# Batch 0 of a Fourier-mixing and gated-FFN kernel: first chunk pair by pair, a new float64 conversion, loads in order of need

## The chip, the cores and the metric

The kernel runs on one core of a Trainium2 chip. The metric is the time of one execution in microseconds (us). The median before the change was 2103.89 us over three runs (2100.69 to 2103.98). Every timed run of this study fell in the fast state. Runs taken once, without rounds, have an unknown state and are named as single runs.

Engine names as the profile has them: PE is TensorE, PEld its weight loads, DVE VectorE, ACT ScalarE, POOL GpSimd, SP SyncE. A trailing q (ACTq) is that engine's instruction stream, not its arithmetic. "PEclk" is the granted TensorE clock as a share of full speed.

## The reference

```python
x: (8, 3008, 256) float32                       # batch, sequence, features
X   = real(fft(fft(x, axis=1), axis=2))         # mixing over sequence, then features
t   = X.reshape(8 * 3008, 256)
out = (sigmoid(t @ w_gate) * (t @ w_val)) @ w_out
# w_gate, w_val: (256, 1536); w_out: (1536, 256); all three arrive as float64
```

## The kernel before

TensorE sums over the sequence with cosine and sine tables ("sequence sums", tiles `ev`, `od`). The feature transform is merged into the gate and value weights (`merge`, tiles `ps`, `pe`, results `G1`, `G2`, `ge`). Then every batch is worked off in chunks of 256 sequence positions. A chunk has six *pairs* of hidden blocks, each pair has two *halves*: `front` (four matmuls into `pa`, four into `pb`), the sums on VectorE, a sigmoid on ScalarE, gating on VectorE and GpSimd, and four halves later `back` (matmuls into `po`).

Before any pair can run, x and the tables have to land, x has to be folded, the sequence sums of batch 0 have to run, and the float64 weights have to become float32 and be merged. The order of batch 0, with cuts marked:

```python
load_x(0)                                        # two halves of x
nc.scalar.dma_start(out=dt, ...)                 # feature table
for t in range(2):
    nc.scalar.dma_start(out=st[:, t], in_=stab[:, t])     # sequence tables
...
for f in fold_ops(0, nc.vector, NQ): f()
seq_start(0)
for blk in range(2):
    for what in range(3):
        seq_group(0, blk, what)()                # 12 sequence sums
load_weights()                                   # all 18 weight tiles, then merged
load_x(1)
e_load()                                         # column 128 of batches 1 to 7
```

One weight tile of 128x512 numbers was converted so (`hi`, `lo` are the two 32-bit words of a float64):

```python
ts(out=expi, in0=hi, scalar1=0x7FF00000, ...)                    # VectorE
nc.gpsimd.tensor_scalar(out=exp, in0=expi, ... mult, add)        # GpSimd: new exponent
nc.gpsimd.tensor_scalar(out=expi, in0=exp, ... max, min)         # GpSimd: clamp
ts(out=mani, in0=hi, ... and, shift)                             # VectorE
ts(out=mani, in0=mani, scalar1=0x3F800000, ... or)               # VectorE
stt(out=man, in0=lo, scalar=2.0 ** -52, in1=man, mult, add)      # VectorE
nc.gpsimd.tensor_tensor(out, man, exp, op=ALU.mult)              # GpSimd
stt(out=out, in0=hi, scalar=-(2 ** 31), in1=out, and, or)        # VectorE: sign
```

The other part that matters is the load of feature column 128 (`HD`), which later batches need on its own. Seven loads, each of 126 x 4 x 6 = 3024 pieces of four bytes, are issued by ScalarE:

```python
def e_load():
    for b in range(1, B):
        nc.scalar.dma_start(out=x8[:, b - 1], in_=xf[b, :, :, :, HD : HD + 1])
```

## Time and profile before

| | before |
|---|---|
| median of 3 runs | 2103.89 us |
| span of the profiled run | 2099.9 us |
| busy: TensorE, VectorE, GpSimd, ScalarE | 96%, 85%, 65%, 23% |
| mean granted clock | 0.984 |
| front of half 10 starts (landmark of the prediction) | 168.47 us |

The busy shares are averages, and they hide where the idle time lies. TensorE's 4% of idle time is about 80 us, and 69 us of it stand before 143 us. Therefore the views to read are the ones of the first 170 us: the slices, the stretch windows, the chain that ended last, and ScalarE's timeline. The prediction shows the lines.

### The profile page before, as it was taken

How to read it: one execution, taken by the hardware profiler on the slowest of the kernel's cores; microseconds unless marked ns; L12 is line 12 of the kernel's file. 1: busy time of each engine (PE TensorE's matmuls, PEld its weight loads, DVE VectorE, ACT ScalarE, POOL GpSimd, SP SyncE). 2: the span in 40 equal slices, each digit the busy share in tenths (PEclk: the TensorE clock that was granted, in tenths of full speed). 3: DMA queues.
4: the chain of work that ended last, by engine and by line, in shares of the span. 5: the costliest groups of instructions: out<-in, count | busy, mean ns of one | idle time of the engine just before them, and what ended most of it. 6: DMA issues, size and time to landing. Idle time of an engine off the chain costs nothing.

```text
span 2099.9 us, 27507 instructions
## 1 busy us (share of the span) xinstructions
PE 2020.0 (96%) x9264; PEld 1757.6 (84%) x9264; DVE 1790.4 (85%) x3263; ACT 479.0 (23%) x842; POOL 1371.0 (65%) x1663
## 2 busy tenths in 40 slices
PE   4749999999999999999999999999999999999998
PEld 2638788988898888988889888988889888898887
DVE  3979877998789978899779987899788997798887
ACT  0112222222222222222222222222222222222222
POOL 0988844687556964589446975569645894565664
PEclk9769999999999999999999999999999999999999
DMA  5350100210002000201002100020002010000001
GB/s 181 104 108 2 30 16 11 70 24 21 11 12 77 25 11 16 74 11 32 14 11 70 34 11 11 16 74 26 11 18 72 10 36 11 11 13 17 11 16 24
DMA packets 132579, 70.96 MB, mean 34 GB/s; under 512 B 124405, under 2 KB 124661, under 8 KB 130172
## 3 DMA queue, kind: packets, MB, share of 16 engines
q1 hardware_dynamic: 110608, 64.27, 10.9%
q10 hardware_dynamic: 21832, 4.94, 1.2%
q8 instruction: 74, 1.21, 0.2%
q14 instruction: 65, 0.53, 0.1%
HBM read 44.50 MB, written 24.68 MB: 33 GB/s over the span
## 4 chain that ended last, share of the span: by engine, by line
PE 74%; POOL 18%; DVE 5%; issue 2%; DMA 1%; ACTq 0%; DVEq 0%; ACT 0%; POOLq 0%
PE po L88 32%; PE pa L88 18%; PE pb L88 18%; PE ev L88 3%; PE od L88 3%; POOL sf L324 2%; POOL sf L323 2%; POOL exp L136 2%; POOL sf L321 2%; POOL sf L325 2%; DMA st<-in_stab_dram 1%; POOL x L211 1%; DVE h L319 1%; POOL x L218 1%; DVE ae L304 1%
## 5 line engine op out<-in xcount | busy, mean ns | idle before, releaser
L443 ACT ACTIVATE z<-z 128x512 f32<-128x512 f32 (+1 forms) x576 | 358.6, 622 | 1316.6 <-DVE z L308 1316.6
L304 DVE SCALAR_TENSOR_TENSOR ae<-ek,ge,pa 128x256 f32<-128x256 f32 (+1 forms) x1152 | 489.9, 466 | 194.2 <-PE pa L88 190.7
L88 PE MATMUL pa<-pk,G 128*128 128x256 f32 (+1 forms) x2304 | 583.1, 375 | 28.7 <-DVE ae L304 28.7
L88 PE MATMUL pb<-qk,G 127*128 127x256 f32 (+1 forms) x2304 | 583.5, 375 | 0.0
L88 PE MATMUL po<-sf,wf 128*128 128x256 f32 (+1 forms) x2304 | 537.4, 375 | 0.6
L88 PEld LDWEIGHTS pa<-pk,G 128*128 128x128 f32 x2304 | 438.3, 190 | 86.2 <-DVE ae L304 29.1
L88 PEld LDWEIGHTS po<-sf,wf 128*128 128x128 f32 x2304 | 435.5, 190 | 55.7 <-POOL sf L325 3.3
L88 PEld LDWEIGHTS pb<-qk,G 127*128 127x128 f32 x2304 | 437.7, 190 | 51.7
L323 POOL TENSOR_TENSOR sf<-h 128x256 f32<-128x256 f32 (+1 forms) x288 | 212.7, 738 | 398.1 <-DVE h L319 398.1
L319 DVE TENSOR_TENSOR h<-z 128x512 f32<-128x512 f32 (+1 forms) x576 | 443.8, 770 | 0.0
L307 DVE TENSOR_TENSOR z<-ae,pb 128x512 f32<-128x512 f32 (+1 forms) x576 | 390.1, 677 | 60.6 <-DVE ae L304 0.9
L88 PE MATMUL po<-h,wf 128*128 128x256 f32 (+1 forms) x1728 | 413.0, 374 | 0.0
L308 DVE TENSOR_TENSOR z<-ae,pb 128x512 f32<-128x512 f32 (+1 forms) x576 | 386.1, 670 | 0.0
L88 PEld LDWEIGHTS po<-h,wf 128*128 128x128 f32 x1728 | 327.5, 189 | 38.6
L321 POOL TENSOR_TENSOR sf<-h 128x256 f32<-128x256 f32 (+1 forms) x288 | 217.5, 755 | 214.9 <-DVE h L319 213.7
L324 POOL TENSOR_TENSOR sf<-sf,h 128x256 f32<-128x256 f32 (+1 forms) x288 | 213.9, 743 | 22.6
L325 POOL TENSOR_TENSOR sf<-h,sf 128x256 f32<-128x256 f32 (+1 forms) x288 | 213.4, 741 | 22.6
L88 PE MATMUL ev<-st,x 126*128 126x377 f32 (+5 forms) x204 | 72.3, 490 | 24.3 <-DMA st<-in_stab_dram 24.3
L360 ACT COPY c<-po 128x512 f32<-128x512 f32 (+1 forms) x144 | 78.5, 579 | 67.9 <-PE po L88 67.9
L367 DVE STREAM_TRANSPOSE os<-c 128x256 f32<-128x256 f32 x192 | 83.5, 436 | 0.0
L88 PEld LDWEIGHTS ev<-st,x 126*128 126x128 f32 (+2 forms) x204 | 37.8, 187 | 46.4 <-DVE x L212 23.4
L389 POOL TENSOR_TENSOR c<-c 128x512 f32<-128x512 f32 (+1 forms) x47 | 74.6, 1586 | 0.0
(68 smaller groups left out, 855.0 us busy)
## 6 DMA issues: line engine op xcount, KB each, us to landing
x<-in_xf_dram SPq DMA_DIRECT2D x16, 1512.0 KB
out_dram<-os SPq DMA_DIRECT2D x288, 64.0 KB
out_dram<-os SPq DMA_DIRECT2D x96, 56.0 KB
ek<-ed SPq DMA_DIRECT2D x7, 752.5 KB
st<-in_stab_dram ACTq DMA_DIRECT2D x2, 2223.7 KB
raw<-in_moe_w_gate_dram SPq DMA_DIRECT2D x6, 512.0 KB
raw<-in_moe_w_val_dram SPq DMA_DIRECT2D x6, 512.0 KB
raw<-in_moe_w_out_dram SPq DMA_DIRECT2D x6, 512.0 KB
```

What stands on the lines that cost most here:

```text
L88: nc.tensor.matmul(o, l, r, start=start, stop=stop, skip_group_check=True)
L304: nc.vector.scalar_tensor_tensor(out=ae[:, g], in0=ek[:, ks], scalar=ge[:, g, f : f + 1], in1=pa[:, g], op0=ALU.mult, op1=ALU.add)
L307: nc.vector.tensor_tensor(z[:, :, 0], ae, pb, op=ALU.add)
L308: nc.vector.tensor_tensor(z[:, :, 1, ::-1], ae, pb, op=ALU.subtract)
L319: nc.vector.tensor_tensor(h[:, fh], z[:, 0], z[:, 1], op=ALU.mult)
L321: tt(s[:, 2], h[:, 0, 0], h[:, 0, 1], op=ALU.subtract)
L323: tt(s[:, 0], h[:, 0, 1], h[:, 1, 1], op=ALU.add)
L324: tt(s[:, 1], s[:, 0], h[:, 0, 0], op=ALU.subtract)
L325: tt(s[:, 3], h[:, 1, 0], s[:, 1], op=ALU.subtract)
L360: nc.scalar.copy(t[:, 2 * j : 2 * j + 2, 0:n], PO[j][:, :, 0:n])
L367: nc.vector.transpose(os_[:, s, 0:nb, h, :], t[:, slot, 0 : nb * TB])
L443: nc.scalar.activation(z[:, 0], z[:, 0], AF.Sigmoid)
```

## The change

The intent is to let the pairs of the first chunk start while weights are still arriving. Weight tiles are reordered so that each pair's gate, value and output tiles come together; two tiles are loaded and converted first of all, three more are converted before the first half, and the other 13 inside the loop. The conversion uses three engines, with a single GpSimd instruction in place of three. x comes in three parts and the tables in four, each cut into a 112-row and a 14-row transfer. Copies of the folded x and of the output weights move from VectorE to ScalarE, and the second batch's x is loaded one chunk later. The diff, cut to its core:

```diff
-    def load_x(b):
+    def rows(out, src):
+        m = NP // 16 * 16                                  # 112 of 126 rows
+        nc.sync.dma_start(out=out[0:m], in_=src[0:m])
+        nc.sync.dma_start(out=out[m:NP], in_=src[m:NP])
+    def load_x(b, nq):
...
+    def weight_round(j):
...
+        nc.scalar.activation(ws, hi.bitcast(F32), AF.Abs)
+        nc.scalar.activation(lo, lo.bitcast(U32), AF.Copy, scale=2.0 ** -29)
+        ts(out=ws, in0=ws, scalar1=2.0 ** -15, scalar2=HUGE, op0=ALU.max, op1=ALU.min)
+        ts(out=wi, in0=wi, scalar1=3, scalar2=0x3FFFFFF8, op0=ALU.logical_shift_left,
+           op1=ALU.bitwise_and)
+        nc.vector.scalar_tensor_tensor(out=wi, in0=hi, scalar=-(2 ** 30), in1=wi,
+                                       op0=ALU.bitwise_and, op1=ALU.bitwise_or)
+        nc.gpsimd.tensor_tensor(wi, wi, lo, op=ALU.add)
...
-        nc.vector.tensor_copy(f[:, 0:2], w[:, :, 0])       # forms of w_out
+        nc.scalar.copy(f[:, 0:2], w[:, :, 0])
...
-    load_weights()
-    load_x(1)
-    e_load()
+    for j in range(2, KEEP):                               # three tiles before half 0
+        weight_round(j)
+    weight_use(2)
...
+    for c in range(1, NPR):
+        i = 2 * (c - 1)                                    # side work of halves i and i + 1
+        at(i, lambda c=c: weight_use(3 * c), lambda c=c: weight_step(3 * c + 2))
+        at(i + 1, lambda c=c: weight_use(3 * c + 1), lambda c=c: weight_use(3 * c + 2))
+        if c + 1 < NPR:
+            at(i, lambda c=c: weight_step(3 * c + 3))
+            at(i + 1, lambda c=c: weight_step(3 * c + 4))
+    i0 = 2 * NPR
+    at(i0 + 1, lambda: load_x(1, 3), e_load)               # column 128 now inside the loop
```

More of the change, by code (lines that the diff above doesn't have):

```diff
@@ L37 @@
 NP = 126
+HUGE = float((2 ** 24 - 1 - 2 ** 20) * 2.0 ** -7)
 @with_exitstack
@@ L94 @@
     X = {}
-    def load_x(b):
+    def rows(out, src):
[3 more added lines that the diff above has]
+    def load_x(b, nq):
         X[b] = xp.tile([NP, 4, NQ, D], F32, name="x4", tag="x4")
-        for h in range(2):
-            nc.sync.dma_start(out=X[b][:, 2 * h : 2 * h + 2], in_=xf[b, :, 2 * h : 2 * h + 2])
+        for q in range(0, NQ, nq):
+            rows(X[b][:, :, q : q + nq], xf[b, :, :, q : q + nq])
     dt = const.tile([P, 2, D], F32, name="dt")
@@ L109 @@
     ed = dram.tile([B - 1, NK], F32, name="ed")
-    load_x(0)
-    nc.scalar.dma_start(out=dt, in_=dtab.rearrange("(c p) d -> p c d", p=P))
-    for t in range(2):
-        nc.scalar.dma_start(out=st[:, t], in_=stab[:, t])
-    def weight_ops(src, out):
-        src = src.rearrange("(c p) f -> p c f", p=P)
-        if src.dtype == F32:
-            return lambda: nc.sync.dma_start(out=out, in_=src), lambda: None
-        raw = zp.tile([P, 2, WC, 2], I32, name="raw", tag="z")
-        man = hp.tile([P, 2, WC], F32, name="man", tag="h")
-        exp = op.tile([P, 2, WC], F32, name="exp", tag="os")
-        lo = raw.bitcast(U32)[:, :, :, 0]
-        hi = raw[:, :, :, 1]
-        mani, expi = man.bitcast(I32), exp.bitcast(I32)
-        ts = nc.vector.tensor_scalar
-        stt = nc.vector.scalar_tensor_tensor
-        def first():
-            nc.sync.dma_start(out=raw.rearrange("p c f w -> p c (f w)"), in_=src.bitcast(I32))
-            ts(out=expi, in0=hi, scalar1=0x7FF00000, scalar2=None, op0=ALU.bitwise_and)
-            nc.gpsimd.tensor_scalar(out=exp, in0=expi, scalar1=8.0, scalar2=-896.0 * 2.0 ** 23,
-                                    op0=ALU.mult, op1=ALU.add)
-            nc.gpsimd.tensor_scalar(out=expi, in0=exp, scalar1=0.0, scalar2=255.0 * 2.0 ** 23,
-                                    op0=ALU.max, op1=ALU.min)
-            ts(out=mani, in0=hi, scalar1=0xFFFFF, scalar2=3, op0=ALU.bitwise_and,
-               op1=ALU.logical_shift_left)
-            ts(out=mani, in0=mani, scalar1=0x3F800000, scalar2=None, op0=ALU.bitwise_or)
-            stt(out=man, in0=lo, scalar=2.0 ** -52, in1=man, op0=ALU.mult, op1=ALU.add)
-            nc.gpsimd.tensor_tensor(out, man, exp, op=ALU.mult)
-        def then():
-            stt(out=out.bitcast(I32), in0=hi, scalar=-(2 ** 31), in1=out.bitcast(I32),
-                op0=ALU.bitwise_and, op1=ALU.bitwise_or)
-        return first, then
@@ new lines, in load_tables, with weight_load @@
+    def load_tables():
+        for t in range(2):
+            for cs in (slice(0, NE), slice(NE, NE + NO)):
+                rows(st[:, t, :, cs], stab[:, t, :, cs])
+    jobs = [(w, c) for c in range(NPR) for w in range(3)]
+    RAW, WS = {}, {}
+    mega = []
+    KEEP = 5
+    def weight_load(j):
+        w, c = jobs[j]
+        src = (moe_w_gate, moe_w_val, moe_w_out)[w]
+        src = src[2 * c * P : 2 * (c + 1) * P, :] if w == 2 else src[:, c * WC : (c + 1) * WC]
+        src = src.rearrange("(c p) f -> p c f", p=P)
+        if j < KEEP:
+            raw = zp.tile([P, 2, WC, 2], I32, name="raw", tag="z")
+            ws = (app if j < 3 else hp).tile([P, 2, WC], F32, name="ws", tag="ae" if j < 3 else "h")
+        else:
+            if not mega:
+                mega.append(xp.tile([P, 12, 2 * WC], F32, name="mega", tag="x4"))
+            r, i = (j - KEEP) % 3 * 2, 6 + (j - KEEP) % 6
+            raw = mega[0][:, r : r + 2].rearrange("p a n -> p (a n)").bitcast(I32).rearrange(
+                "p (c f w) -> p c f w", c=2, w=2)
+            ws = mega[0][:, i].rearrange("p (c f) -> p c f", c=2)
+        WS[j] = ws
+        if src.dtype == F32:
+            nc.sync.dma_start(out=ws, in_=src)
+        else:
+            RAW[j] = raw
+            nc.sync.dma_start(out=raw.rearrange("p c f w -> p c (f w)"), in_=src.bitcast(I32))
@@ new lines, in weight_round @@
+    def weight_round(j):
+        if j not in RAW:
+            return
+        raw = RAW.pop(j)
+        lo, hi = raw[:, :, :, 0], raw[:, :, :, 1]
+        ws = WS[j]
+        wi = ws.bitcast(I32)
+        ts = nc.vector.tensor_scalar
+        nc.scalar.activation(ws, hi.bitcast(F32), AF.Abs)
[6 more added lines that the diff above has]
+        nc.gpsimd.tensor_tensor(wi, wi, lo, op=ALU.add)
@@ L149, in merge, with weight_use @@
+    def weight_use(j):
+        w, c = jobs[j]
+        (forms(WS.pop(j), c) if w == 2 else merge(WS.pop(j), w, c))
     def merge(ws, g, c):
@@ L168, in forms @@
         sub = lambda o, a, b: nc.gpsimd.tensor_tensor(o, a, b, op=ALU.subtract)
-        nc.vector.tensor_copy(f[:, 0:2], w[:, :, 0])
-        nc.vector.tensor_copy(f[:, 2], w[:, 1, 1])
+        nc.scalar.copy(f[:, 0:2], w[:, :, 0])
+        nc.scalar.copy(f[:, 2], w[:, 1, 1])
         sub(f[:, 4], w[:, 0, 1], w[:, 0, 0])
@@ L174, in forms @@
         sub(f[:, 3], w[:, 1, 0], f[:, 5])
-    def load_weights():
-        jobs = []
-        for c in range(NPR):
-            for g, w in enumerate((moe_w_gate, moe_w_val)):
-                jobs.append((w[:, c * WC : (c + 1) * WC], g, c))
-        for c in range(NPR):
-            jobs.append((moe_w_out[2 * c * P : 2 * (c + 1) * P, :], None, c))
-        rest = []
-        for src, g, c in jobs:
-            ws = app.tile([P, 2, WC], F32, name="ws", tag="ae")
-            first, then = weight_ops(src, ws)
-            first()
-            for f in rest:
-                f()
-            use = (lambda ws=ws, c=c: forms(ws, c)) if g is None else (
-                lambda ws=ws, g=g, c=c: merge(ws, g, c))
-            rest = [then, use]
-        for f in rest:
-            f()
     W = {}
@@ L205, in point, with first @@
             tt(x4[:, i, q, 1:D], x4[:, i, q, 1:D], x4[:, j, q, D - 1 : 0 : -1], op=ALU.add)
-        def first(i, j):
-            tt(x4[:, i, :, 0], x4[:, i, :, 0], x4[:, j, :, 0], op=ALU.add)
+        def first(i, j, q):
+            tt(x4[:, i, q, 0], x4[:, i, q, 0], x4[:, j, q, 0], op=ALU.add)
         def feat(v, r, q):
@@ L212, in feat, with kind @@
             tt(v[:, q, 1:HD], v[:, q, 1:HD], v[:, q, D - 1 : HD : -1], op=ALU.add)
+        parts = [(x4[:, 1 + 2 * blk], x4[:, 2 * blk]) for blk in range(2)]
         qs = [slice(q, q + nq) for q in range(0, NQ, nq)]
-        for i in (0, 2):
-            ops += [lambda i=i, q=q: point(i, i + 1, q) for q in qs]
-            ops.append(lambda i=i: first(i, i + 1))
-        ops += [lambda q=q: tt(x4[:, 1, q], x4[:, 0, q], x4[:, 2, q], op=ALU.add) for q in qs]
-        ops += [lambda q=q: tt(x4[:, 3, q], x4[:, 0, q], x4[:, 2, q], op=ALU.subtract) for q in qs]
-        for blk in range(2):
-            v, r = x4[:, 1 + 2 * blk], x4[:, 2 * blk]
+        def kind(q):
+            two = [[lambda i=i: point(i, i + 1, q)] for i in (0, 2)]
+            return two + [[lambda: tt(x4[:, 1, q], x4[:, 0, q], x4[:, 2, q], op=ALU.add)],
+                          [lambda: tt(x4[:, 3, q], x4[:, 0, q], x4[:, 2, q], op=ALU.subtract)]] + [
+                [lambda v=v, r=r: feat(v, r, q)] for v, r in parts]
+        if b:
+            for n, group in enumerate(zip(*[kind(q) for q in qs])):
+                ops += [f for fs in group for f in fs]
+                if n < 2:
+                    ops.append(lambda n=n: first(2 * n, 2 * n + 1, slice(0, NQ)))
+        else:
+            for q in qs:
+                for n, fs in enumerate(kind(q)):
+                    ops += fs
+                    if n < 2:
+                        ops.append(lambda n=n, q=q: first(2 * n, 2 * n + 1, q))
+        for blk, (v, r) in enumerate(parts):
+            W[b, blk] = (v[:, :, 0:HD], r[:, :, 0 : HD - 1])
             if b == 0:
                 we = cp.tile([NP, NQ, P], F32, name="we", tag="c7")
-                ops.append(lambda we=we, v=v: eng.tensor_copy(
+                ops.append(lambda we=we, v=v: nc.scalar.copy(
                     we, v[:, :, HD : HD + 1].to_broadcast([NP, NQ, P])))
-            ops += [lambda v=v, r=r, q=q: feat(v, r, q) for q in qs]
-            W[b, blk] = (v[:, :, 0:HD], r[:, :, 0 : HD - 1]) + ((we,) if b == 0 else ())
+                W[b, blk] += (we,)
         return ops
@@ L258, in seq_group @@
     def seq_group(b, blk, what):
-        rows = HD - 1 if what == 1 else P
-        return half(lambda q: W[b, blk][what][:, q, :], PQE[b][what], blk, what == 1, rows)
+        return half(lambda q: W[b, blk][what][:, q, :], PQE[b][what], blk, what == 1,
+                    HD - 1 if what == 1 else P)
     ER = []
@@ L395, in finish @@
             lambda: store(1)])
-    for f in fold_ops(0, nc.vector, NQ):
-        f()
+    nc.scalar.dma_start(out=dt, in_=dtab.rearrange("(c p) d -> p c d", p=P))
+    for j in range(2):
+        weight_load(j)
+    load_x(0, 2)
+    load_tables()
+    for j in range(2, KEEP):
+        weight_load(j)
+    for j in range(2):
+        weight_round(j)
+    for f in fold_ops(0, nc.vector, 2):
+        f()
+    for j in range(2):
+        weight_use(j)
     seq_start(0)
-    for blk in range(2):
-        for what in range(3):
-            seq_group(0, blk, what)()
-    load_weights()
-    load_x(1)
-    e_load()
+    for blk, what in ((0, 0), (0, 2), (1, 0), (1, 2), (0, 1), (1, 1)):
+        seq_group(0, blk, what)()
+    for j in range(2, KEEP):
+        weight_round(j)
+    weight_use(2)
+    for j in range(KEEP, KEEP + 3):
+        weight_load(j)
     per = 2 * NPR * len(chunks)
@@ L416, in split, with weight_step @@
         at(i, lambda: at(i + 1, f(*args)))
+    def weight_step(j):
+        weight_round(j)
+        if j + 3 < len(jobs):
+            weight_load(j + 3)
+    for c in range(1, NPR):
[7 more added lines that the diff above has]
+    at(i0 + 1, lambda: load_x(1, 3), e_load)
     for b in range(B - 1):
@@ L420, with folds @@
         if b:
-            at(s0 + 1, lambda b=b: load_x(b + 1))
-        def folds(s0=s0, b=b):
+            at(s0 + 1, lambda b=b: load_x(b + 1, 3))
+        f0, g0, gs = (s0 + 9, s0 + 36, 8) if b else (i0 + 9, i0 + 36, 7)
+        def folds(f0=f0, b=b):
             for j, f in enumerate(fold_ops(b + 1, nc.gpsimd, 2)):
-                at(s0 + 9 + j, f)
-        at(s0 + 8, folds)
-        at(s0 + 33, lambda b=b: seq_start(b + 1))
+                at(f0 + j, f)
+        at(f0 - 1, folds)
+        at(g0 - 3, lambda b=b: seq_start(b + 1))
         for j in range(4):
-            split(s0 + 36 + 8 * j, seq_group, b + 1, j // 2, j % 2)
-    at(20, e_fold)
-    split(26, e_rows, 0)
-    split(28, e_rows, 1)
-    at(30, e_out)
+            split(g0 + gs * j, seq_group, b + 1, j // 2, j % 2)
+    at(i0 + 22, e_fold)
+    split(i0 + 28, e_rows, 0)
+    split(i0 + 30, e_rows, 1)
+    at(i0 + 32, e_out)
     fresh = None
```

## The prediction

> **What bounds the kernel now.** I first read the busy tenths of the page and the stretch windows. Columns of a window: length, then busy us (and instructions) of TensorE, its weight loads, VectorE, ScalarE and GpSimd, then granted clock, DMA share, GB/s.
>
> ```profile
> PE   4749999999999999999999999999999999999998
> POOL 0988844687556964589446975569645894565664
> PEclk9769999999999999999999999999999999999999
> 10.00:20.00 10.00, 0.00 (x0) 0.00 (x0) 5.01 (x6) 0.00 (x0) 0.00 (x0) 1.00 0.89 319
> 80.00:90.00 10.00, 7.86 (x38) 6.95 (x38) 9.86 (x13) 2.15 (x9) 9.50 (x7) 0.81 0.36 105
> 120.00:130.00 10.00, 0.00 (x0) 0.00 (x0) 6.92 (x12) 0.00 (x0) 9.59 (x12) 0.50 0.95 276
> 160.00:170.00 10.00, 10.00 (x48) 8.79 (x47) 9.69 (x18) 2.41 (x4) 5.10 (x7) 1.00 0.00 1
> ```
>
> From about 143 us on TensorE never rests; before that it is idle or underfed. So the whole change can only act on the start. The chain that ended last says what fills it (start, us, what):
>
> ```profile
> 1.98 28.69 DMA st<-in_stab_dram
> ...
> 90.52 1.31 POOL ws L142
> 91.82 0.09 issue
> 91.91 0.69 POOL exp L134
> 92.67 2.28 POOL exp L136
> ...
> 143.10 2.08 PE pa L88 x4
> ...
> 168.47 0.86 PE pa L88 x4
> ```
>
> First the tables land (30.7 us), then twelve sequence sums on TensorE run to 50 us, then GpSimd converts 18 weight tiles at 4.5 us each (0.69 + 2.28 + 1.31 and gaps), and only at 143.1 do the pairs run. Counting two halves a pair, two fronts had been slipped in before; a pair takes 6.48 us (0.86 four times, 1.30, 1.73), and the front of half 10 starts at 168.47. That is my landmark: everything behind it stays TensorE work.
>
> Two more views. The by-form list from 51 to 142 us gives the cost of a conversion's operations (count, busy us, mean ns, idle before):
>
> ```profile
> L142 POOL TENSOR_TENSOR ws<-man,exp 128x512 f32<-128x512 f32 x18 | 23.5, 1305 | 1.5
> L140 DVE TENSOR_SCALAR man<-man 128x512 int32<-128x512 int32 x18 | 19.6, 1089 | 0.6
> L145 DVE SCALAR_TENSOR_TENSOR ws<-raw,ws 128x512 int32<-128x512 int32 x18 | 18.0, 1001 | 9.5 <-POOL ws L142 9.5
> L138 DVE TENSOR_SCALAR man<-raw 128x512 int32<-128x512 int32 x18 | 15.0, 835 | 0.0
> ```
>
> And ScalarE's timeline shows something now hidden: the seven loads of column 128 (4-byte pieces) hold its instruction stream for 26 us, beside the GpSimd chain that ends at 140.5 anyway.
>
> ```profile
> 110.90 26.25 ACTq L267 DMA_DIRECT2D x<-in_xf_dram  x7
> 137.24 1.28 ACT L443 ACT_TABLE_LOAD   x1 [26.19 <-DMA x<-in_xf_dram]
> ```
>
> **What the Trainium skill says.**
> - "SBUF — State Buffer", Who interferes with whom: VectorE in a two-port mode, or with two SBUF inputs, and GpSimd lock each other out for a whole instruction. The trace agrees: a TENSOR_SCALAR of 128x512 takes 0.42 to 0.43 us at 118.4, when it meets no lock, and 0.84 to 1.09 on average over the conversion.
> - "TensorE: Matmul & The Clock Gate", What's actually happening: the clock halves after an idle window of about 3.4 us and returns after a busy one. Here it halved about 2.4 us after TensorE stopped (114.4), and after the restart at 143.1 the 2 us windows (0.50, 0.50, 0.61, 1.00) give 4.5 us at half clock, a loss of 2.2.
> - "DMA: Bandwidth & Descriptors", Why a DMA increments its semaphore by 16: a transfer uses the largest number of engines up to 16 that divides its outer dimensions, so 126 partitions use 14. The DMA share of 0.88 to 0.89 while x and the tables stream agrees (14/16 = 0.875). The new split into 112 and 14 rows gives the busiest engine 8 rows in place of 9.
> - "ScalarE: Activation LUTs", Step-by-step: every function has the same rate per element. So Abs and Copy of 128x512 should take sigmoid's 0.62 us of this trace; no run of before has them.
>
> **The change, part by part.**
>
> *Loads.* Two weight tiles now go first, then x in three parts, then the tables in four. Until the first table quarter 0.26 + 1.05 + 3.10 + 1.14 = 5.55 MB are due; at 319 GB/s times 9/8, that is 360, plus 2.5 us: 18 us. The folds, in three parts of about 4.1 us (twelve operations at the rates of the present ones), finish at about 21; then ScalarE's copies also free the four PSUM banks the first two merges hold. The remaining tables land by 28, never late. Twelve groups of 1.90 us, plus 2.2 for the cold clock, end at about 46.5 instead of 50.
>
> *Conversion.* Per tile GpSimd drops from three operations (4.3 us) to one integer add (as L142, 1.3); VectorE from five to three (two TENSOR_SCALAR, one SCALAR_TENSOR_TENSOR: 1.6 us free of locks, from 0.45 + 0.46 + 0.69 at 118.4; 2.9 at the averages above; GpSimd now being busy some 60% instead of 95%, I take 2.3); ScalarE gains two of 0.62. Three tiles are converted before half 0: VectorE 47.5 to 54.4, then its front operations (two ae, two z, 2.3 together), the table load 1.3, sigmoid 0.63, three copies of merged weights 0.8: 59, say 58.5.
>
> *Pair by pair.* Per pair TensorE has 6.5 + two merges of 2.75 (present trace, full clock) = 12.0; VectorE 6.1 + 3 x 2.3 = 13.0; GpSimd 3 x 1.3 + forms 2.4 + gating 3.0 = 9.3; ScalarE 7.3. If these overlapped perfectly, 13 us. But the in-order lists of the changed program make a ring: ScalarE does Abs and Copy only behind the sigmoid and the merged copies of that half; VectorE does the front of the next half only behind those roundings. From the merged copies of an even half: Abs 0.7, two roundings 4.6, front 2.3, sigmoid 0.7, copies 0.9, wf copies 0.65, Abs 0.65, one rounding 2.2, front 2.3, sigmoid 0.7, copies 0.9: 16.6 us. TensorE waits in it about 4 us for the odd half's copies, enough to lose its clock; then front (cold), back, merge end 17.5 instead of 15.4 after the mark. I take 17 us a pair. Four such pairs lead to half 8: 58.5 + 68 = 126.5. Half 8 has one rounding left, half 9 none: + 0.7 + 2.2 + 2.3 + 0.7 + 0.8 = 6.7. Front of half 10: 133.2, against 168.5, 35.3 earlier.
>
> *Column 128.* Its seven loads now stand in ScalarE's list behind the sigmoid of half 13, inside the loop that TensorE bounds. Alone, one took 2.19 us (the last, behind the other traffic); seven are 15.4, less some 2.4 that stay queued: ScalarE issues nothing for about 13 us. TensorE has front 14, back 10, front 15, back 11, front 16 to do meanwhile, then needs the output banks that ScalarE empties at the chunk's end: 7.6 us of work. It resumes at about 14.7: a hole near 6.7, and 2.2 for the clock: 8.9 us given back.
>
> *Rest.* The second batch's x and folds move one chunk later, with 60 halves instead of 72 to hide in; GpSimd has room (26 to 48 of 50 us). Zero.
>
> Sum: 35.3 - 8.9 = 26.4 earlier; 2103.9 - 26.4 = 2077.5, rounded 2077.
>
> **The rivals.**
> 1. *The engines overlap as their sums allow:* 13 us a pair and no clock loss. Front 10 at 58.5 + 52 + 6 = 116.5, gain 52, less the hole 43: 2061. For it: all four sums are below 13. Against: the ring, and the locks, which in the present conversion keep VectorE at 9.86 of 10.
> 2. *The loads of column 128 cost nothing:* they queue without holding ScalarE, or are through sooner with free DMA engines; with 17 us a pair, 2069, with 13 a pair 2052. For it: in the present trace they shared the DMA with 4.7 MB. Against: the last one alone still took 2.19 us.
> 3. *The clock stays half:* TensorE needs up to 24 us of work a pair, so a pair takes 20 to 21. Front 10 at about 147, gain 21 less 9: 2092. For it: the present conversion, with gaps of 1.8 us, runs at 0.66 to 0.89. Against: gaps are fewer and the work between them denser.
> 4. *A lost overlap in steady state* (batch 0's squeezed side work): some us, nothing in the profile near its limit.
>
> **Range and chances.** The pair time (14 to 20 us, four times) is worth 24 us, the hole 5 to 12. Together 2060 to 2092. Faster by over 2% needs less than 2061.8: rival 1 or 2 nearly pure, 0.17. Slower by 2% would need new stalls of 68 us: 0.01.
>
> **What would show it.** After: sequence sums from about 21 to 46 us; conversion operations at 0.6 (ScalarE), 1.3 (GpSimd); pairs 17 us apart, with TensorE waiting on ScalarE's merged copies and a clock below 1; front 10 near 133; one gap of sigmoids of about 13 us about 13 us later, with a TensorE hole of 6 to 7 in it, waiting for ScalarE; then 100% to the end. Wrong if the pairs come every 13 us, if the integer add on GpSimd is much slower than 1.3, or if no hole follows the column loads.

## The result

The median after the change is 2075.58 us over four runs (2074.76 to 2076.9), against 2103.85 for the kernel before in the same comparison. Ratios in this document are the mean time of one kernel's fast runs over that of the other's of the same rounds, so they are not quite the ratio of the medians that are quoted. Here the ratio is 0.987, with a 95% interval of 0.9853 to 0.9887: 1.3% less time, which counts as "same" at the 2% line. The profiled spans are 2099.9 and 2072.8 us, 27.1 apart, where the prediction had 26.4. The mean clock went from 0.984 to 0.988.

The busy tenths of the page of the kernel after, in 40 slices of 51.8 us each:

```profile
PE   7789999999999999999999999999999999999998
POOL 0546944696558944687556974579545885565654
```

TensorE's first slice went from 4 to 7, the second stayed at 7, and the third went from 4 to 8. That third slice is 104 to 155 us: the old idle time before the pairs is gone from it, but it holds a new hole. GpSimd's second slice fell from 9 to 5.

TensorE's timeline shows where the sequence sums start. The bracket holds the idle time just before and what ended it:

```profile
24.83 3.83 PE L92 MATMUL ev<-st,x 126*128 126x377 f32 x6 [6.03 <-ACT ge L189]
```

They start at 24.83 (predicted 21), released by ScalarE's last copy of merged weights and not by a table. ScalarE's list has two copies of folded x ahead of the merged copies, and these could start only at 22.67, behind VectorE's folds. The folds began at 10.99 and ended at 24.9. Their first operation in VectorE's timeline, with the idle time before it:

```profile
10.99 1.42 DVE L212 TENSOR_TENSOR x<-x 126x510 f32<-126x510 f32 x1 [0.54 <-DMA x<-in_xf_dram]
```

So x was waited for only 0.54 us. Until 10.44 VectorE was still rounding the first two weight tiles, which stand ahead of the folds in its list.

The groups by line and shape between 62 and 130 us give the cost of the new conversion (count, busy us, mean ns, idle before and what ended it):

```profile
L170 POOL TENSOR_TENSOR mega<-mega 128x512 int32<-128x512 int32 x13 | 16.9, 1297 | 19.0 <-issue 9.6 <-ACT mega L164 5.8 <-DVE mega L168 3.5
L166 DVE TENSOR_SCALAR mega<-mega 128x512 int32<-128x512 int32 x13 | 10.8, 830 | 0.4
L168 DVE SCALAR_TENSOR_TENSOR mega<-mega 128x512 int32<-128x512 int32 x13 | 9.0, 692 | 0.4
L163 ACT ACTIVATE mega<-mega 128x512 f32<-128x512 f32 x13 | 9.0, 690 | 0.0
L165 DVE TENSOR_SCALAR mega<-mega 128x512 f32<-128x512 f32 x13 | 6.5, 499 | 17.7 <-ACT mega L163 15.2 <-POOL sf L347 2.5
```

GpSimd's integer add takes 1.30 us, as predicted. VectorE's three operations add up to 0.50 + 0.83 + 0.69 = 2.02 us a tile, where 2.3 was predicted. The 0.83 of L166 is a mean of unlike cases: 0.43 us where no GpSimd instruction ran beside it, 0.56 to 0.84 beside other GpSimd work, and 1.38 to 1.41 each time it fell beside the integer add of the tile before. The last row shows VectorE waiting 15.2 us in all for ScalarE's Abs.

That wait is one link of the ring that the prediction described. A piece of the chain that ended last, over one odd half (start, us, what):

```profile
99.88 0.63 ACT z L495
100.51 0.26 ACT G L187
...
101.10 0.31 ACT wf L196
...
101.61 0.59 ACT mega L163
...
102.22 0.63 DVE mega L165
...
102.88 0.57 DVE mega L166
...
103.47 0.69 DVE mega L168
104.16 0.80 DVE ae L326 x2
...
105.05 0.69 DVE z L329
105.74 0.61 DVE z L330
...
106.37 0.63 ACT z L495
```

It runs from one sigmoid to the next without TensorE: sigmoid, merged copies, copies of the output weights, Abs, rounding on VectorE, front sums on VectorE, sigmoid. Sigmoids of even halves start at 60.71, 75.40, 90.53, 106.37 and 121.63, that is 60.92 / 4 = 15.23 us a pair. The front of half 10 starts at 129.50, 39.0 us earlier than before.

Then comes the hole. ScalarE's timeline behind the sigmoid of half 13, and the chain over the same time:

```profile
142.52 0.63 ACT L495 ACTIVATE z<-z 128x512 f32<-128x512 f32 x1 [2.40 <-DVE z L330]
142.54 16.72 ACTq L289 DMA_DIRECT2D x<-in_xf_dram  x7
159.30 0.37 ACT L370 COPY c<-po 128x256 f32<-128x256 f32 x1 [16.16 <-issue]
```

```profile
143.15 0.84 ACTq L289
...
144.02 4.01 ACTq L289
...
148.06 2.23 ACTq L289
...
157.05 2.21 ACTq L289
...
159.30 0.38 ACT c L370
...
159.73 3.08 PE po L92 x6
```

ScalarE can do nothing from 143.15 to 159.26 because its instruction stream is issuing the seven loads of column 128 ("<-issue" means that the copy waited for no other engine). TensorE runs out of work, then continues at half clock. Its timeline and its stretch window (length; busy us of TensorE, weight loads, VectorE, ScalarE, GpSimd; clock; DMA share; GB/s):

```profile
159.73 3.08 PE L92 MATMUL po<-h,wf 128*128 128x256 f32 x6 [8.80 <-ACT c L370]
150.00:160.00 10.00, 1.20 (x6) 0.74 (x5) 0.00 (x0) 0.70 (x2) 0.00 (x0) 0.73 0.75 5
```

The whole path moves 5 GB/s in this window while the DMA engines are busy 75% of the time: many tiny pieces. Of the 39.0 us won by half 10, the span kept 27.1; 11.9 were given back.

### The profile page after: what moved, and what is told of

Same layout as the page of the kernel before. It is cut to its first block, busy times and chain, and to the rows that moved or that the text cites. A ratio compares the mean times of both kernels' runs of the same rounds, so it can differ in the third digit from the quotient of the medians.

```text
span 2072.8 us, 27549 instructions
## 1 busy us (share of the span) xinstructions
PE 2023.2 (98%) x9264; PEld 1757.7 (85%) x9264; DVE 1750.4 (84%) x3233; ACT 502.2 (24%) x892; POOL 1316.3 (64%) x1627
## 4 chain that ended last, share of the span: by engine, by line
PE 72%; POOL 14%; DVE 6%; issue 2%; ACTq 1%; ACT 0%; DVEq 0%; POOLq 0%
PE po L92 31%; PE pa L92 18%; PE pb L92 17%; PE ev L92 3%; PE od L92 3%; POOL sf L346 2%; POOL sf L345 2%; POOL sf L343 2%; POOL sf L347 2%; DVE ae L326 2%; DVE h L341 1%; POOL x L218 1%; POOL x L226 1%; POOL x L219 1%; DVE z L330 1%
## 5 line engine op out<-in xcount | busy, mean ns | idle before, releaser
L92 PE MATMUL od<-st,x 126*128 126x377 f32 (+5 forms) x204 | 70.1, 479 | 0.0
```

What stands on the lines that cost most here:

```text
L92: nc.tensor.matmul(o, l, r, start=start, stop=stop, skip_group_check=True)
```

## The experiments

All runs gave the right output. Runs without an interval are single ones.

Two theories stood. **Mine:** the ring of in-order lists sets the pair time, and the issue of the column loads costs some 9 to 12 us. **The rivals:** the engines' sums or the clock set the pair time; and the TensorE hole comes from something else, such as the second batch's x. A third question was whether the new loads are really faster.

### e_sp: the column loads issued by SyncE

```diff
-            nc.scalar.dma_start(out=x8[:, b - 1], in_=xf[b, :, :, :, HD : HD + 1])
+            nc.sync.dma_start(out=x8[:, b - 1], in_=xf[b, :, :, :, HD : HD + 1])
```

> The changed kernel with the seven column-128 loads issued from the sync engine's queue instead of ScalarE's. Theory A (ScalarE's instruction stream is held while its own queue issues them; 16.1 us from 143.2 to 159.3 in the changed kernel's trace): no ScalarE gap, no TensorE hole near 151 to 160, about 11.5 us less: 2062 to 2066. Rival B (the hole comes from the DMA being full, and something else that needs a DMA is late): the hole stays or moves, 2073 to 2077.

Measured: 2064.07 us (2063.06 to 2064.84), ratio 0.9816 (0.98 to 0.9833), as theory A expected. ScalarE's timeline at the place of the hole:

```profile
144.20 0.63 ACT L495 ACTIVATE z<-z 128x512 f32<-128x512 f32 x1 [2.40 <-DVE z L330]
146.60 0.37 ACT L370 COPY c<-po 128x256 f32<-128x256 f32 x1 [1.77 <-PE po L92]
147.66 0.63 ACT L495 ACTIVATE z<-z 128x512 f32<-128x512 f32 x1 [0.69 <-DVE z L330]
```

The copy follows the sigmoid by 2.4 us instead of 16.8, and the hole is gone with the same bytes and pieces moved. So it was the issue on ScalarE's stream, and its price was 2075.58 - 2064.07 = 11.5 us. SyncE's stream was held for 24.2 us instead, and TensorE did not wait for it. Whether a stream is held by the work of issuing so many pieces or by a queue that is full is not shown.

### before_e_sp: the same edit in the kernel before

The edit is the one of e_sp, made in the old kernel.

> The kernel before with the same single edit. Theory A with 'hidden behind the GpSimd chain': no change, 2102 to 2106. Rival (these loads cost the kernel before as well): 2088 to 2095.

Measured: 2102.8 us, ratio 0.9999 (0.9984 to 1.0014). In the old order the loads held ScalarE for 26 us and cost nothing, because everything waited for GpSimd's conversions until 140.5 anyway. The change moved the loads from a hidden place to an exposed one.

### ring: ScalarE's part of a conversion one half earlier

`weight_round` is cut in two. The Abs and Copy of a tile are emitted one half ahead; nothing else moves.

```diff
+    def weight_act(j):                  # Abs and Copy, once per tile
...
     def weight_round(j):
+        weight_act(j)
-        nc.scalar.activation(ws, hi.bitcast(F32), AF.Abs)
-        nc.scalar.activation(lo, lo.bitcast(U32), AF.Copy, scale=2.0 ** -29)
...
+    for j in range(KEEP, KEEP + 2):     # ahead of half 0
+        weight_act(j)
...
+            at(i, lambda c=c: weight_act(3 * c + 4))
+            at(i + 1, lambda c=c: weight_act(3 * c + 5))
+                at(i + 1, lambda c=c: weight_act(3 * c + 6))
```

> The changed kernel with the two ScalarE operations of each conversion put into ScalarE's list one half earlier, so that VectorE finds Abs done when it comes to a rounding; nothing else moved. Theory A (the ring ScalarE-VectorE-TensorE sets the 15.2 us pairs): pairs of about 13 us, the sum of VectorE's work; front of half 10 near 120 instead of 129.6; 2064 to 2068. Rival C (VectorE's locks with GpSimd set the pair): pairs stay at 14.5 to 15.5, 2073 to 2076. Rival D (TensorE's halved clock sets it): pairs stay above 15.

Measured: 2063.42 us (2061.77 to 2063.65), a little less than the 2064 to 2068 expected, ratio 0.9813 (0.9799 to 0.9828; whether that is 2% is unclear). Even sigmoids start at 61.59, 72.05, 85.14, 98.31 and 111.61. That is 50.0 us for four pairs instead of 60.9; the last three take 13.1 to 13.3 each. The front of half 10 starts at 119.02, 10.5 us earlier than in the kernel after. The waits between 62 and 122 us (who waits for what: us, times, longest), first of the kernel after and then of this run:

```profile
ACT z L495 <- DVE z L330: 34.3, 8, 5.3
DVE mega L165 <- ACT mega L163: 13.0, 7, 3.2
```

```profile
ACT z L513 <- DVE z L339: 19.8, 9, 3.8
```

VectorE's wait for Abs, 13.0 us in the first, is no longer among the waits of the second, and the sigmoid waits 14.5 us less. A stretch of one pair in this run:

```profile
85.00:98.00 13.00, 13.00 (x70) 11.63 (x69) 12.59 (x20) 6.85 (x16) 9.48 (x12) 1.00 0.39 121
```

VectorE is busy 12.59 of 13 us, and TensorE never rests and keeps its clock. This is the prediction's first rival, 13 us a pair, and it came true as soon as the ring was opened. So the ring was the bound in the kernel after, and neither the engines' sums nor the clock. (The clock has a part in the gain, because it stays full once the gaps are short. But the kernel after needed 14.7 us even for a pair that kept the full clock, the third, from 92.87 to 107.60.) The hole behind half 13 is still there (ScalarE held from 132.66 to 148.0, TensorE idle 8.02).

### ring_e_sp: both edits

> Both edits of the changed kernel together. If both theories A hold, the gains add: 2052 to 2057 and no hole. If only the column loads matter: 2062 to 2066.

Measured: 2054.03 us (2052.19 to 2054.88), ratio 0.9769 (0.9754 to 0.9784), which counts as faster, clock 0.993. The two gains nearly add: against the kernel after, the ratio falls by 0.0054 (e_sp), 0.0057 (ring) and 0.0101 (both). Hence they are separate causes.

### conv_only and conv_only_e_sp: the new conversion in the old order

conv_only is the kernel before with the body of the new conversion (the six new operations of the diff above) and an empty second step; loads, order and the rest are old. conv_only_e_sp issues the column loads from SyncE as well.

> The kernel before with only the new conversion (five operations on ScalarE, VectorE, one GpSimd add) put into its old order: all 18 tiles, then the pairs; column-128 loads on ScalarE's queue behind the conversions. The GpSimd chain of 4.5 us a tile should become about 3.2 us for the 12 gate and value tiles and 3.7 for the 6 output tiles (add 1.3 and forms 2.4), about 60 us in place of 90, so that the column loads (16 us or more, beside the second batch's x) are no longer hidden: first sigmoids near 130 instead of 144. Theory A (conversion is over half of the gain of the change): 2086 to 2092. Theory B (the order is what pays): 2098 to 2104.

> The kernel before with the new conversion in the old order, and the column-128 loads on the sync engine's queue. Theory A (with the conversion at about 60 us the column loads were what hid the rest of its gain, 127.1 minus 109.9 us of ScalarE's list): 2069 to 2074, that is, better than the whole change as it stands, and the pair-by-pair order is worth only 5 to 10 us beyond it. Rival B (something else holds the pairs back until about 125 us): 2082 to 2087.

Measured: conv_only 2086.35 us (2085.41 to 2088.79), ratio 0.9924 (0.9907 to 0.994). conv_only_e_sp 2078.55 us (2077.89 to 2079.69), ratio 0.989 (0.9875 to 0.9904). ScalarE's timelines, of conv_only and then of conv_only_e_sp:

```profile
110.27 16.71 ACTq L261 DMA_DIRECT2D x<-in_xf_dram  x6
127.08 1.28 ACT L437 ACT_TABLE_LOAD   x1 [16.58 <-issue]
```

```profile
120.71 1.28 ACT L437 ACT_TABLE_LOAD   x1 [7.08 <-DVE z L302]
```

With the old order kept, the new conversion ended 26 us earlier (last integer add at 114.4 us, against the last multiplication at 140.4), and the old place of the column loads at once became exposed: the table load for the sigmoid waited 16.58 us for the issue. This is the same cost at another place. conv_only came out as its theory A had it. My expectation for conv_only_e_sp was 2069 to 2074, and it missed. Taking the issue away moved the table load by only 6.4 us, because the chain of the six output tiles (3.9 us a tile, to 117.5) then held the fronts until 119.30. The step that I had left out is that conv_only already slipped two fronts in during the hold.

By ratios, of 2103: the conversion alone, off ScalarE's stream, gives 0.011 or 23 us; the order pair by pair with its loads gives a further 0.0074 or 16 us (e_sp against conv_only_e_sp); the column loads' new place takes back 0.0054 or 11 us.

### norows, bigst, norows_bigst, norows_timed: the shape of the loads

norows moves all 126 rows in one transfer. bigst keeps the split into rows but not the one of the tables' columns. norows_bigst drops both. norows_timed is norows with rounds.

```diff
-        nc.sync.dma_start(out=out[0:m], in_=src[0:m])        # norows
-        nc.sync.dma_start(out=out[m:NP], in_=src[m:NP])
+        nc.sync.dma_start(out=out, in_=src)
...
-            for cs in (slice(0, NE), slice(NE, NE + NO)):    # bigst
-                rows(st[:, t, :, cs], stab[:, t, :, cs])
+            rows(st[:, t], stab[:, t])
```

> The changed kernel with x and the tables loaded as one 126-row transfer each piece, not 112 + 14 rows. My theory for the slow loads of the changed kernel (about 250 GB/s from 8 to 42 us where 360 was expected): the pieces are short (2 KB and 1.5 KB runs), so this run stays near 220 to 250 GB/s. Rival: the 14-row remainder costs it; then 300 GB/s or more and the tables land before 36 us.

> The changed kernel with each table loaded whole (18 KB runs in place of 1.5 KB), rows still split. Short-run theory: above 320 GB/s in the table phase, all tables in by about 34 us. Rival (remainder rows): no change, 42 us. In both cases the time stays within 2 us of the changed kernel if, as I think, the tables are not waited for; if the loads matter, it gains 3 us or more.

> Both edits: whole tables, no row split. If the split is worth what the engine count says (16 of 16 against 14 of 16), the table phase is about 12% slower than in the run with whole tables and split rows; if not, the same.

> The changed kernel without the row split, now timed. If the split costs (254 against 305 GB/s in the start, and 16.2 against 13.7 us of held ScalarE): 2071 to 2073. If the single run was luck: 2075 to 2077.

| run | time, us | GB/s from 8 to 24 us | DMA share |
|---|---|---|---|
| before | 2103.89 | 323 | 0.91 |
| after | 2075.58 | 254 | 1.08 |
| norows (single) | 2071.73 | 305 | 0.93 |
| norows_timed | 2071.8 | 329 | 0.93 |
| bigst (single) | 2079.68 | 265 | 1.08 |
| norows_bigst (single) | 2074.42 | 316 | 0.99 |

The windows from 8 to 24 us, of the kernel after and of norows_timed:

```profile
8.00:24.00 16.00, 9.77 (x32) 8.22 (x32) 15.01 (x31) 1.71 (x3) 2.26 (x2) 0.92 1.08 254
```

```profile
8.00:24.00 16.00, 9.58 (x32) 8.12 (x32) 15.46 (x31) 1.98 (x4) 2.83 (x2) 0.91 0.93 329
```

With the rows split, the DMA engines are busier (a share of 1.08 against 0.93), and they move less. My theory after the result was that the tables' short column runs were to blame, so I expected norows to stay at 220 to 250 GB/s. It had 305 with the same runs, and its timed twin 329 (two traces of one kernel, so readings differ by this much); bigst, for which that theory wanted above 320, had 265. So that theory fell for this window: splitting the rows is what makes the loads slow. norows_bigst, expected to be some 12% slower than bigst if the split is worth something, was faster. From 24 to 32 us, however, norows_timed ran at 262 GB/s and norows_bigst at 337, so the cut of the columns may cost something late in the loads; no run followed this up.

In time it matters little: norows_timed has the ratio 0.986 (0.9843 to 0.9876), whose interval overlaps that of the kernel after. By medians it is 3.8 us less (2071 to 2073 was expected), by ratios 2, so at most a few us. The faster loads did not start TensorE earlier: its first sequence sum starts at 24.80 in norows_timed and at 24.83 in the kernel after. ScalarE is held by the column loads for 14.4 us in place of 16.7. bigst costs 4.1 us against the kernel after, where I had expected a difference of at most 2. TensorE shows why, in its timeline:

```profile
30.26 3.56 PE L92 MATMUL ev<-st,x 126*128 126x377 f32 x6 [13.95 <-DMA st<-in_stab_dram]
```

The first sequence sum now waits for a table twice as large, and starts 5.4 us later. The cut of the columns is useful, the cut of the rows is not.

### split_late: the 112-row pieces first, the 14-row ones last

```diff
-        for t in range(2):
-            for cs in (slice(0, NE), slice(NE, NE + NO)):
-                rows(st[:, t, :, cs], stab[:, t, :, cs])
+        for ps in (slice(0, 112), slice(112, NP)):
+            for t in range(2):
+                for cs in (slice(0, NE), slice(NE, NE + NO)):
+                    nc.sync.dma_start(out=st[ps, t, :, cs], in_=stab[ps, t, :, cs])
```

> The changed kernel with the four 112-row pieces of the tables first and the four 14-row remainders after them. If remainders between the pieces are what slows the loads, the 112-row phase runs above 320 GB/s. If the 112-row transfers themselves are slow, it stays near 250. Theory so far: none preferred; TensorE will wait for the remainders, so the time will be worse in either case.

The question was whether the small 14-row transfers in between slow the large ones. Measured: a single run of 2090.37 us. Its window from 16 to 32 us, in which 112-row pieces of the tables move, and the same window of the kernel after:

```profile
16.00:32.00 16.00, 0.75 (x7) 0.66 (x6) 9.04 (x22) 2.78 (x8) 0.00 (x0) 0.63 1.09 248
```

```profile
16.00:32.00 16.00, 9.97 (x31) 6.52 (x30) 9.68 (x23) 3.25 (x9) 0.00 (x0) 0.79 1.10 239
```

248 against 239 GB/s: the 112-row transfers are slow by themselves, and this rival fell too. (The run is slow because no table is complete until the last pieces land; TensorE worked 0.75 of these 16 us.) Why they are slow stays open.

### best: ring, e_sp and no row split

> The changed kernel with ScalarE's part of the conversion a half earlier, the column-128 loads on the sync engine's queue, and no row split. The column loads no longer hold ScalarE, so the split should matter little here: 2051 to 2055 (2054.0 with the split).

Measured: 2052.72 us (2051.35 to 2054.28), ratio 0.9766 (0.9752 to 0.9781), which counts as faster than the kernel before by 2.3%. It is also below the kernel after, 2052.72 against 2075.58, with intervals far apart. Over ring_e_sp (0.9769) the whole rows add nothing that can be resolved. Its even sigmoids at the start of two successive pairs, in ScalarE's timeline:

```profile
84.33 0.63 ACT L511 ACTIVATE z<-z 128x512 f32<-128x512 f32 x1 [0.95 <-DVE z L337]
...
97.41 0.63 ACT L511 ACTIVATE z<-z 128x512 f32<-128x512 f32 x1 [0.30 <-DVE z L337]
```

They are 13.1 us apart, so the pairs are as short as in ring.

## Why the prediction was right

The prediction of 2077 us, with a change of less than 2% as the likely outcome, held: 2075.58. Step by step:

- **Only the start can move.** Right. The front of half 10 came 39.0 us earlier, the span is 27.1 us shorter, and nearly all of the 11.9 between them is one hole of 8.8 us with its cold clock (half clock until about 164.8 us, a loss of about 2.5).
- **Loads, folds and sequence sums (21 to 46.5).** The chain was right (folds, ScalarE's copies, sums), the size off: 24.83 to 49.38. "At 319 GB/s times 9/8, that is 360" was wrong, for the loads ran at 254 and the tables landed at about 42 us instead of 28. But that is not what made the sums late: VectorE waited for x 0.54 us, TensorE for no table, and norows_timed with 329 GB/s started the sums at 24.80. The terms that failed are VectorE's. To end at 21, three parts of 4.1 us would have to start at 8.7; the two roundings ahead of them, which the prediction leaves out there, ran until 10.44, and the folds took 13.9 us instead of 12.3.
- **Conversion and first half.** Merged copies of half 0 were done at 61.9, predicted 58.5: 3.4 us late. Most of it is the 3 us of the start, carried on; besides, the prediction's own items add up to 59.4, and it took 58.5. Three conversions on VectorE took 6.5 us (50.57 to 57.05), predicted 6.9. Abs took 0.69 us on average in the loop, where the prediction took the sigmoid's 0.62 from an equal rate. Its reading that a TENSOR_SCALAR "meets no lock" at 118.4 is not sure: GpSimd's L136 was recorded from 117.52 to 119.72. The clear case is L166 in the kernel after, 0.43 us alone and about 1.4 beside the integer add.
- **Pair by pair, 17 us.** The ring was the mechanism; ring and its waits show it. From the end of the merged copies of one even half to the next (61.94, 76.62, 92.87, 107.60, 123.76), the prediction's own mark, the pairs took 14.7, 16.2, 14.7 and 16.2 us, so four took 6.2 us less than 68. The terms that were too large: the roundings (the two of an even half 4.02 to 4.58, predicted 4.6; the one of an odd half 1.76 to 1.87, predicted 2.2), the merged copies (0.6 where they did not wait for TensorE, predicted 0.9), the Abs on the path (0.59, predicted 0.65 to 0.7), and the clock lost in every pair. TensorE did lose it, but only in about every second pair, the long ones: the windows of 8 us from 84 to 124 have granted clocks of 0.65, 1.00, 1.00, 0.85 and 0.73. From the merged copies of half 8 (123.76) to the front of half 10 (129.50) it took 5.7 us, predicted 6.7.
- **Column 128, 8.9 us given back.** Right in kind, shown by e_sp; it was 11.9 by the two differences and 11.5 by e_sp. ScalarE was held 16.1 us, predicted 13, and TensorE's hole was 8.80, predicted 6.7 (the prediction's own 14.7 less 7.6 would be 7.1). The step that failed was to subtract 2.4 us that "stay queued". The second load alone took 4.01 us while the second batch's x was still landing; the last five took 2.21 on average, close to the 2.19 of the prediction.
- **Sum.** The errors nearly cancelled: +3.4 (start), -6.2 (pairs), -1.0 (halves 8 and 9), +3.0 (hole), about -0.7 us together, so the measured gain in span is 27.1 where 26.4 was predicted. The right total owes something to luck; the single terms were off by up to 6 us.
- **Rivals.** The first (13 us a pair) was wrong for this kernel and right for one in which the ring is opened. The second (free column loads) fell by e_sp. The third (half clock throughout) fell: the clock was 1.00 in three of the seven windows of 8 us from 68 to 124. The fourth left no trace.

## What to carry to other kernels

When side work is spread over in-order engines, follow one item from engine to engine: if each engine takes it up only behind its own part of the present step, the latencies add up to a ring even though no engine is busy all the time (here, from 68 to 124 us, TensorE was busy 81% and VectorE 72%). Starting the first engine's part one step earlier then opens the ring (here 12 us). A load of many tiny pieces blocks the stream of the engine that issues it, so issue it from an engine that nothing waits for; a place at which it is hidden today stops being hidden when the chain beside it gets shorter. A higher share of busy DMA engines is not more bytes per second: measure the GB/s.

## What the Trainium skill lacked or had wrong

- "DMA: Bandwidth & Descriptors", Why a DMA increments its semaphore by 16: the rise of the DMA share from 0.91 to 1.08, when 126 rows became 112 and 14, fits the page's number of engines, but no trace here counts them (norows_bigst, with 126 rows, had 0.99). The page doesn't say that more engines can move less. Here loads cut into 112 and 14 rows ran at 238 to 265 GB/s from 8 to 24 us, and loads of 126 rows at 305 to 333. I had drawn a gain of 9/8 from the page; no run here shows the reason.
- "DMA: Bandwidth & Descriptors", Issuing engines are not separate DMA queues: it calls the time on the sequencer that initiates a DMA "usually small relative to the DMA itself". For loads of 3024 four-byte pieces it was not small: seven of them held ScalarE's stream for 16.1 us, the last five 2.21 us each on average. The page gives no time for what the issue of so many short pieces costs the engine that issues them.
- "TensorE: Matmul & The Clock Gate", What's actually happening: the page gives about 3.4 us of idle time before the clock halves. In the kernel before it halved about 2.4 us after TensorE stopped; in the kernel after, TensorE came out of a gap of 1.53 us at full clock (two matmuls in 0.70 us, at 100.82) and out of one of 1.50 us at half clock (two in 1.22 us, at 113.77). No single gap length explains the runs here. The page calls its window free-running; whether that explains the difference, no run here tests.
